# Another unit order for one token group, weight splits moved beside it, and an output block in two halves

## The chip, the cores and the metric

The kernel runs on one core of a Trainium2 chip, all in one launch. The metric is the device time of that launch in microseconds. Beside the times there is one profiled execution, with a trace of every engine: TensorE (PE, its weight loads PEld), VectorE (DVE), ScalarE (ACT), GpSimd (POOL) and the DMA queue of SyncE (SP).

## What is computed

The reference, cut to what matters (float32 in and out; 1152 tokens, 512 features):

```python
x = attention(q, k, v)                 # 2 x 8 heads, 576 positions, 32 keys per query (every 4th for half the heads)
h = x @ w_in                           # MoE1: 512 -> 2048
g = h * np.tanh(np.log1p(np.exp(h)))
x = g @ w_out                          # 2048 -> 512
p = domain_probs / domain_probs.sum(-1, keepdims=True)
for e in range(4):                     # MoE2: four experts, 512 -> 1024 -> 512
    out += p[:, e:e + 1] * (np.maximum(x @ w1[e], 0) @ w2[e])
```

## The kernel before

Every matrix product is done in three matmuls: each operand is split into a high part (`hi`, an ACT copy to the matmul's float format) and the rest (`lo`, a subtraction), and hi·hi, hi·lo and lo·hi are added up in PSUM. A **split** is thus one ACT instruction and one subtraction on DVE or POOL (`split`, L541 to L543).

**Attention** ends about 90 us in and isn't touched.

**MoE1** has 16 units; a unit `u` is 128 columns of `w_in` with the 128 rows of `w_out` that belong to them, 1024 columns of hi and of lo. They are decoded and split while token group 0 runs (`dec_dve`, `dec_act`) and then stay in SBUF: units 0 to 3 in `wxh`/`wxl`, unit 4 in `late[0:2]`, units 5 to 15 one behind the other in `late[2:4]` (11264 columns). Tokens come in three groups of 512, 320 and 320. Group 0 has one unit in a step, groups 1 and 2 have two. A step (`Step1`) is `first` (24 matmuls of L497, into banks 6 and 7), `act` (the Mish, ACT L502), `split` (ACT L505, DVE L506) and `second` (24 matmuls of L517, into four banks kept for the whole group). The loop at L830 emits, for each step i, `first` of i, `second` of i - 1, then `act` and `split` of i, and then what the table `beside` lists for it: splits that MoE2 will need. NSB is the number of the first step of group 2, its last is NSB + 7. `y_out` copies a group's four banks out, in turn on ACT and DVE.

**MoE2** computes x·w1 by a scheme with 7 products in place of 8 (A11·B11, S1·T1, S2·T2, ...: sums of blocks of w1, and of x). An expert's weights come in four pairs (`p`), each 256 hidden columns. A pair is prepared by

- `prep_a`: splits of A12 and A22 (ACT 512 and 256 wide, DVE), then four POOL sums in place (L654 to L657),
- `prep_s`: split of the four sums (ACT 1024 wide, DVE), then the load of the next pair's w1,
- `prep_w2`: split of w2 (ACT 1024 wide, POOL), then the load of the next pair's w2.

The result takes 2816 columns of `late[2:4]`, pair p from column 2816·p on, so over MoE1's units: pair 0 over units 5 to 7, pair 1 over 7 to 10, pair 2 over 10 to 13, pair 3 over 13 to 15. Expert 0's pairs can be written only where group 2 has already used those units. The staging buffers `stage1` (w1) and `stage2` (w2) hold one pair each.

Work on tokens goes by `Group`: expert e, token set j (256 or 320 columns a product), pair p. `first_a` runs five of the products, `mid` and `first_b` the rest with Relu and split, `second` multiplies by w2 into `accs`, banks 1 to 4 or 1 to 5, which are kept over the four pairs, and `finish` (after pair 3) adds prob times the bank to the output rows (DVE L764) and stores them (SP L766). Products use three banks: a, b, c, which are 6, 7, 0. In `first_a`, ACT copies bank a away (L710, L714) before the next product goes into it:

```python
            self.prod(self.a, "A11", "B11", True)
            self.prod(self.b, "S1", "T1", True)
            ACT.activation(p1, self.a, AF.Copy)
            ACT.activation(self.cb[:, 2 * N:3 * N], self.b, AF.Copy)
            self.prod(self.a, "S2", "T2")
```

The loop at L856 emits for group i: `first_a`, the first half of `second` of group i - 1 (for i = 0 MoE1's last `second` and `y_out(2)`), `mid`, the work in `slots[i, 0]`, `first_b`, the second half of that `second`, the work in `slots[i, 1]`. Nothing reorders what is emitted: each engine takes its instructions in this order. The last group's `second` stands at the end (L873 to L878): per output block of 128 tokens six matmuls, then `finish` of the block.

Of the kernel before, what the change touches and what calls it, by code (L numbers as in the profile page):

```python
# [23 lines left out]
def kernel(  # L24
# [13 lines left out]
    PE, ACT, DVE, POOL, SP = nc.tensor, nc.scalar, nc.vector, nc.gpsimd, nc.sync  # L38
# [3 lines left out]
    DM = out.shape[1]  # L42
    NT = B * S
    NE = w1.shape[0]
    NF1 = w_in.shape[1] // 128
    NF2 = w1.shape[2] // 128
    NUA = 4
# [15 lines left out]
    def nm(s):  # L63
        uid[0] += 1
        return f"{s}{uid[0]}"

    def bank(n):
        return ps.tile([128, 512], F32, tag=f"bank{n}", name=nm("bank"))
# [158 lines left out]
    for lo in (0, 32):  # L227
        m = msk[lo:lo + 32, :]
# [23 lines left out]
    t = bank(7)  # L252
# [223 lines left out]
    yacc = {}  # L476

    class Step1:
# [29 lines left out]
        def second(self):  # L508
            if self.grp not in yacc:
                yacc[self.grp] = [bank(b)[:, 0:self.w] for b in ((0, 1, 2, 3), (4, 5, 0, 1), (2, 3, 4, 5))[self.grp]]  # L510
            for i, u in enumerate(self.us):
                wh, wl = units[u]
                g = slice(self.w * i, self.w * (i + 1))
                for d in range(4):
                    s = slice(512 + 128 * d, 640 + 128 * d)
                    for k, (a, x) in enumerate(((wh, self.ghi), (wl, self.ghi), (wh, self.glo))):
                        PE.matmul(yacc[self.grp][d], a[:, s], x[:, g], start=u == 0 and k == 0,  # L517
                                  stop=u == NF1 - 1 and k == 2)

    steps = [Step1(f, 0, [f]) for f in range(NF1)]  # L520
    NSA = len(steps)
    for g in (1, 2):
        for f in range(0, NF1, 2):
            steps.append(Step1(len(steps), g, [f, f + 1]))
    NS1 = len(steps)
    NSB = (NSA + NS1) // 2

# [25 lines left out]
    NP2 = NF2 // 2  # L553
# [43 lines left out]
    def set0_t42(k):  # L597
        h, l, o = ((xh, xl, 1536), (wxh, wxl, 1024))[k]
        split(h[:, o:o + 512], l[:, o:o + 512], rawf[1][:, 512 * k:512 * k + 512], DVE)
# [4 lines left out]
    def set1_b(m):  # L604
        o = slice(xb + 2 * n1 * m, xb + 2 * n1 * (m + 1))
        split(xh[:, o], xl[:, o], y1[(0, 1, 3)[m]], DVE)
# [20 lines left out]
    def pair_at(n):  # L627
        return divmod(n, NP2) if n < NE * NP2 else None
# [7 lines left out]
    def load_w2(n):  # L636
        if pair_at(n):
            e, p = pair_at(n)
            SP.dma_start(out=stage2.rearrange("p (h d) -> p h d", h=2),
                         in_=w2[e, 256 * p:256 * (p + 1), :].rearrange("(h p) d -> p h d", p=128))  # L640
# [5 lines left out]
    def prep_a(n):  # L646
        o = PW * (n % NP2)
        r = stage1.rearrange("p (c f m) -> p c f m", c=4, f=2)
        a12 = [w[:, o:o + 512].rearrange("p (c m) -> p c m", c=4) for w in late[2:4]]
        a22 = [w[:, o + 512:o + 768].rearrange("p (c m) -> p c m", c=2) for w in late[2:4]]  # L650
        split(*a12, r[:, :, 0], DVE)
        split(*a22, r[:, 2:4, 1], DVE)
        a11, a12, a21, a22 = blocks()
        POOL.tensor_tensor(out=a22, in0=a21, in1=a22, op=ALU.add)  # L654
        POOL.tensor_tensor(out=a21, in0=a11, in1=a21, op=ALU.subtract)
        POOL.tensor_tensor(out=a11, in0=a22, in1=a11, op=ALU.subtract)
        POOL.tensor_tensor(out=a12, in0=a12, in1=a11, op=ALU.subtract)  # L657

    def prep_s(n):
        o = PW * (n % NP2) + 768  # L660
        split(late[2][:, o:o + 1024], late[3][:, o:o + 1024], stage1, DVE)
        load_w1(n + 1)
        ready.add(("s", n))

    def prep_w2(n):
        o = PW * (n % NP2) + 1792
        split(late[2][:, o:o + 1024], late[3][:, o:o + 1024], stage2, POOL)
        load_w2(n + 1)
        ready.add(("w2", n))
# [8 lines left out]
    class Group:  # L678
# [22 lines left out]
        def first_a(self):  # L701
            assert ("s", self.e * NP2 + self.p) in ready
            N = self.N
            self.a, self.b, self.c = (bank(m)[:, 0:N] for m in (6, 7, 0))
            self.cb = rawf[2][:, 0:3 * N]
            p1, u2 = (late[4][:, 320 * i:320 * i + N] for i in range(2))
            self.u2 = u2
# [5 lines that stand above are left out]
            self.prod(self.c, "A12", "B21", True)  # L713
            ACT.activation(u2, self.a, AF.Copy)  # L714
            self.prod(self.a, "S3", "T3")
            DVE.tensor_tensor(out=self.cb[:, 0:N], in0=self.c, in1=p1, op=ALU.add)  # L716
            DVE.tensor_tensor(out=self.cb[:, 2 * N:3 * N], in0=self.a, in1=self.cb[:, 2 * N:3 * N], op=ALU.add)
# [25 lines left out]
        def second(self, f, which=slice(None)):  # L743
            assert ("w2", self.e * NP2 + self.p) in ready
            o = PW * self.p + 1792 + 512 * f
            wh, wl = (w[:, o:o + 512] for w in late[2:4])
            hi, lo = self.g[f]
            for acc, t, cols in self.accs()[which]:
                s = slice(128 * t, 128 * t + 128)
                for i, (x, a) in enumerate(((hi, wh), (hi, wl), (lo, wh))):  # L750
                    PE.matmul(acc, x[:, s], a[:, cols], start=self.p == 0 and f == 0 and i == 0,  # L751
                              stop=self.p == NP2 - 1 and f == 1 and i == 2)

        def finish(self, which=slice(None)):
            if self.p != NP2 - 1:
# [32 lines left out]
    for s in range(-2, NA - 2):  # L788
# [32 lines left out]
              NSA + 2: [lambda: set0_b("B22"), set0_sums, normalise_prob],  # L821
              NSA + 4: [lambda: set0_t42(0)],
              NSB + 1: [set0_t13, lambda: load_w1(0)],
              NSB + 2: [lambda: set0_t42(1), lambda: load_w2(0)],
              NSB + 3: [lambda: set1_b(0), lambda: set1_b(1)],
              NSB + 4: [lambda: prep_a(0)],
              NSB + 5: [lambda: prep_s(0), lambda: prep_w2(0)],
              NSB + 6: [lambda: prep_a(1)],
              NSB + 7: [lambda: prep_s(1), lambda: prep_w2(1)]}
    for i in range(2, NS1):  # L830
        if i > 2:
            steps[i].first()
# [8 lines left out]
    for e in range(NE):  # L841
        for j in range(2):
            for p in range(NP2):
                groups.append(Group(len(groups), e, j, p))
    NG2 = len(groups)

    slots = {(0, 0): [lambda: prep_a(2)], (0, 1): [lambda: prep_s(2), lambda: prep_w2(2)],
             (1, 0): [lambda: prep_a(3)], (1, 1): [lambda: prep_s(3), lambda: prep_w2(3)],
             (2, 0): [lambda: set1_b(2), lambda: set1_sums(0)], (2, 1): [lambda: set1_sums(1), lambda: set1_t("T1")],
             (3, 0): [lambda: set1_t("T3"), lambda: set1_t("T4")], (3, 1): [lambda: set1_t("T2")]}  # L850
    for e in range(1, NE):
        for p in range(NP2):
            n, g = e * NP2 + p, 2 * NP2 * (e - 1) + NP2 + p + 1
# [17 lines left out]
        for do in slots.get((i, 1), ()):  # L871
            do()
    g = groups[-1]  # L873
    n = len(g.accs())
    for t in range(n):
        for f in range(2):
            g.second(f, slice(t, t + 1))
        g.finish(slice(t, t + 1))  # L878
# [32 lines left out]
```

## Time and profile before

| | us |
|---|---|
| three runs | 669.08, 670.16, 671.54 (median 670.16) |
| the profiled execution, its own time | 668.4 |
| its span, first to last instruction | 666.6 |
| TensorE busy | 636.1 |
| DVE, ACT, POOL busy | 290.3, 275.3, 158.8 |
| mean granted clock of TensorE | 0.994 of 2.4 GHz |

The span is what the trace shows; the rest of the execution's own time lies around it. Busy times are of one engine each and overlap. A matmul's row lasts longer than the distance to the next one, since they are pipelined; how fast TensorE goes is read from the distance of the starts. A wait is shown in square brackets behind the instruction that had to wait, with what ended it.

### The profile page before, as it was taken

Reading aid. Unit: us, or ns where it says so; the run is one execution under the profiler, and the core shown is the slowest. Engines: PE = TensorE matmul, PEld = TensorE weight load, DVE = VectorE, ACT = ScalarE, POOL = GpSimd, SP = SyncE. Lnnn points to the kernel's source line nnn. Section 1 sums busy time; section 2 is a strip of 40 time slices with the busy share of each in tenths; the row PEclk is TensorE's granted clock in tenths of the full one; section 3 lists DMA queues with packets and bytes.
Section 4 is the critical chain, followed back from the end, with each engine's and each line's share of the span. In section 5 each row is a group of like instructions: output and inputs, shape, how many; then the busy total and the mean of one; then the engine's idle time right before and its main releaser. Section 6 shows DMA issues by size and latency. Waiting matters only on the chain.

```text
span 666.6 us, 10149 instructions
## 1 busy us (share of the span) xinstructions
PE 636.1 (95%) x4148; PEld 564.7 (85%) x4148; DVE 290.3 (44%) x490; ACT 275.3 (41%) x553; POOL 158.8 (24%) x170
## 2 busy tenths in 40 slices
PE   7676899999999999979999999999999999999997
PEld 4455678888999999969998889998889998898986
DVE  3577876661311223345444452444632544623323
ACT  7797666662322234443244432334422344322210
POOL 8011245550300003345033410043400134300000
PEclk9998999999999999989999999999999999999999
DMA  9999356640000012222003210021210022000102
GB/s 182 221 205 206 98 160 190 188 126 0 1 1 1 1 64 64 64 63 64 1 32 94 64 64 1 0 64 64 64 63 1 1 78 85 28 1 1 63 1 79
DMA packets 47310, 45.82 MB, mean 69 GB/s; under 512 B 12192, under 2 KB 39968, under 8 KB 47264
## 3 DMA queue, kind: packets, MB, share of 16 engines
q1 hardware_dynamic: 47264, 45.18, 25.6%
q8 instruction: 32, 0.52, 0.3%
q14 instruction: 14, 0.11, 0.1%
HBM read 42.81 MB, written 2.36 MB: 68 GB/s over the span
## 4 chain that ended last, share of the span: by engine, by line
PE 86%; ACT 4%; POOL 3%; DMA 2%; DVE 2%; issue 1%; SPq 0%; POOLq 0%; ACTq 0%; DVEq 0%
PE bank L751 30%; PE bank L698 27%; PE bank L517 14%; PE bank L497 14%; DMA raw<-in_moe_w_in_dram 1%; DMA nat<-in_q_dram 1%; ACT qkD L338 1%; ACT qkP L338 1%; ACT xh L420 1%; POOL vP L205 1%; POOL vD L212 0%; PE bank L320 0%; DVE xl L424 0%; DVE scr L150 0%; ACT pr L365 0%
## 5 line engine op out<-in xcount | busy, mean ns | idle before, releaser
L698 PE MATMUL bank<-xh,late 128*128 128x256 f32 (+1 forms) x512 | 121.1, 298 | 5.0 <-ACT late L710 3.6
L698 PEld LDWEIGHTS bank<-xh,late 128*128 128x128 f32 x512 | 88.6, 188 | 9.5 <-ACT late L710 5.1
L698 PE MATMUL bank<-wxh,late 128*128 128x320 f32 (+1 forms) x384 | 95.3, 298 | 0.0
L751 PE MATMUL bank<-late,gh 128*128 128x512 f32 x288 | 89.8, 393 | 0.0
L497 PE MATMUL bank<-xh,late 128*128 128x320 f32 (+1 forms) x288 | 76.3, 338 | 0.0
L698 PE MATMUL bank<-xl,late 128*128 128x256 f32 (+1 forms) x256 | 75.5, 295 | 0.0
L517 PE MATMUL bank<-gh,late 128*128 128x320 f32 (+1 forms) x288 | 72.6, 338 | 0.0
L654 POOL TENSOR_TENSOR raw<-raw 128x256 f32<-128x256 f32 x16 | 11.7, 734 | 238.4 <-DVE late L543 238.4
L698 PEld LDWEIGHTS bank<-wxh,late 128*128 128x128 f32 x384 | 68.3, 189 | 0.0
L506 DVE TENSOR_TENSOR gl<-scr,gh 128x512 fp32r<-128x512 f32 (+1 forms) x32 | 25.0, 780 | 88.7 <-ACT gh L505 88.7
L751 PEld LDWEIGHTS bank<-late,gh 128*128 128x128 f32 x288 | 52.8, 190 | 9.7
L502 ACT ACTIVATE scr<-bank 128x320 f32<-128x320 f32 (+1 forms) x48 | 23.4, 492 | 88.1 <-PE bank L497 88.1
L716 DVE TENSOR_TENSOR raw<-bank,late 128x256 f32<-128x256 f32 (+1 forms) x32 | 14.6, 457 | 101.2 <-PE bank L698 94.1
L751 PE MATMUL bank<-late,gl 128*128 128x512 f32 x144 | 57.0, 396 | 0.0
L698 PE MATMUL bank<-wxl,late 128*128 128x256 f32 (+1 forms) x192 | 56.6, 295 | 0.0
L542 ACT ACTIVATE late<-raw 128x512 fp32r<-128x512 f32 (+1 forms) x64 | 48.2, 783 | 19.9 <-PE bank L751 16.8
L497 PEld LDWEIGHTS bank<-xh,late 128*128 128x128 f32 x288 | 50.7, 188 | 4.3
L517 PEld LDWEIGHTS bank<-gh,late 128*128 128x128 f32 x288 | 50.1, 188 | 4.2
L751 PE MATMUL bank<-late,late 128*128 128x512 f32 x216 | 52.6, 391 | 0.0
L543 POOL TENSOR_TENSOR late<-raw,late 128x1024 fp32r<-128x1024 f32 x16 | 38.7, 2419 | 57.1 <-ACT late L542 57.1
L698 PEld LDWEIGHTS bank<-xl,late 128*128 128x128 f32 x256 | 48.3, 189 | 2.5
L497 PE MATMUL bank<-xl,late 128*128 128x320 f32 (+1 forms) x144 | 48.6, 338 | 0.0
(140 smaller groups left out, 1164.1 us busy)
## 6 DMA issues: line engine op xcount, KB each, us to landing
raw<-in_moe_w_dram SPq DMA_DIRECT2D x32, 512.0 KB, 3.5
raw<-in_moe_w_in_dram SPq DMA_DIRECT2D x16, 512.0 KB, 4.1
raw<-in_moe_w_out_dram SPq DMA_DIRECT2D x16, 512.0 KB, 3.6
out_dram<-scr SPq DMA_DIRECT2D x9, 256.0 KB, 2.1
nat<-in_k_dram SPq DMA_DIRECT2D x8, 256.0 KB, 5.6
nat<-in_q_dram SPq DMA_DIRECT2D x8, 256.0 KB, 6.2
vD<-in_v_dram SPq DMA_DIRECT2D x8, 192.0 KB, 7.0
vP<-in_v_dram SPq DMA_DIRECT2D x8, 160.0 KB, 6.5
```

The costliest lines, as they stand in the source:

```text
L205: POOL.memset(vP[64 * j:64 * j + 64, :, blk, 1 - j, :], 0.0)
L338: ACT.activation(*move(g, par, j), AF.Copy)
L497: PE.matmul(h, a[:, c, :], x[:, c, :], start=c == 0 and k == 0, stop=c == 3 and k == 2)
L502: ACT.activation(self.hc[:, self.w * i:self.w * (i + 1)], h, AF.Mish)
L506: DVE.tensor_tensor(out=self.glo, in0=self.hc, in1=self.ghi.bitcast(F32), op=ALU.subtract)
L517: PE.matmul(yacc[self.grp][d], a[:, s], x[:, g], start=u == 0 and k == 0, stop=u == NF1 - 1 and k == 2)
L542: ACT.activation(hi, src, AF.Copy)
L543: eng.tensor_tensor(out=lo, in0=src, in1=hi.bitcast(F32), op=ALU.subtract)
L654: POOL.tensor_tensor(out=a22, in0=a21, in1=a22, op=ALU.add)
L698: PE.matmul(out, w, x(k), start=first and k == 0 and i == 0, stop=k == 1 and i == 2, skip_group_check=not first)
L716: DVE.tensor_tensor(out=self.cb[:, 0:N], in0=self.c, in1=p1, op=ALU.add)
L751: PE.matmul(acc, x[:, s], a[:, cols], start=self.p == 0 and f == 0 and i == 0, stop=self.p == NP2 - 1 and f == 1 and i == 2)
```

## The change

Four things are changed. Token group 2 takes its units in the order 0, 1, 5 to 15, 2, 3, 4, so that `late[2:4]` comes free from the front two steps earlier (the `start` and `stop` of the accumulation follow that order). Pairs 0, 1 and 2 of MoE2 are prepared in the steps NSB + 2 to NSB + 7 instead of pairs 0 and 1 in NSB + 4 to NSB + 7; pair 3 goes to `slots[0, 1]` and `slots[1, 1]`; the two splits `set1_b` go from one step to two others. Group 1 (n = 1) has bank 5 for its bank a. And the last output block is accumulated, finished and stored in two column halves.

```diff
-                        PE.matmul(yacc[self.grp][d], a[:, s], x[:, g], start=u == 0 and k == 0,
-                                  stop=u == NF1 - 1 and k == 2)
-
-    steps = [Step1(f, 0, [f]) for f in range(NF1)]
+                        PE.matmul(yacc[self.grp][d], a[:, s], x[:, g], start=u == UORD[self.grp][0] and k == 0,
+                                  stop=u == UORD[self.grp][-1] and k == 2)
+    UORD = [list(range(NF1)), list(range(NF1)), [0, 1, *range(NUA + 1, NF1), *range(2, NUA + 1)]]
+    steps = [Step1(f, 0, [f]) for f in UORD[0]]
...
-            steps.append(Step1(len(steps), g, [f, f + 1]))
+            steps.append(Step1(len(steps), g, UORD[g][f:f + 2]))
...
-            self.a, self.b, self.c = (bank(m)[:, 0:N] for m in (6, 7, 0))
+            self.a, self.b, self.c = (bank(m)[:, 0:N] for m in (5 if self.n == 1 else 6, 7, 0))
...
-              NSB + 2: [lambda: set0_t42(1), lambda: load_w2(0)],
-              NSB + 3: [lambda: set1_b(0), lambda: set1_b(1)],
-              NSB + 4: [lambda: prep_a(0)],
-              NSB + 5: [lambda: prep_s(0), lambda: prep_w2(0)],
-              NSB + 6: [lambda: prep_a(1)],
-              NSB + 7: [lambda: prep_s(1), lambda: prep_w2(1)]}
+              NSB + 2: [lambda: set0_t42(1), lambda: load_w2(0), lambda: prep_a(0)],
+              NSB + 3: [lambda: prep_s(0), lambda: prep_w2(0)],
+              NSB + 4: [lambda: prep_a(1), lambda: set1_b(0)],
+              NSB + 5: [lambda: prep_s(1), lambda: prep_w2(1), lambda: set1_b(1)],
+              NSB + 6: [lambda: prep_a(2)],
+              NSB + 7: [lambda: prep_s(2), lambda: prep_w2(2)]}
...
-    slots = {(0, 0): [lambda: prep_a(2)], (0, 1): [lambda: prep_s(2), lambda: prep_w2(2)],
-             (1, 0): [lambda: prep_a(3)], (1, 1): [lambda: prep_s(3), lambda: prep_w2(3)],
+    slots = {(0, 1): [lambda: prep_a(3)], (1, 1): [lambda: prep_s(3), lambda: prep_w2(3)],
...
-    n = len(g.accs())
-    for t in range(n):
+    accs = g.accs()
+    acc, t, _ = accs.pop()
+    accs += [(acc[:, c], t, c) for c in (slice(0, DM // 2), slice(DM // 2, DM))]
+    for t in range(len(accs)):
```

Lines 698, 710, 722, 732, 764 and 766 of the kernel before are 700, 712, 724, 734, 767 and 769 of the changed one.

How the instructions move is shown at three places. The first is ACT from `y_out(2)`'s last copy (L537) to p1 of group 1 (L710), before (`raw0` is stage1, `raw1` stage2, `late2` the hi parts, `late4` holds p1):

```order
L537 ACTIVATE scr_75<-bank168_2206 128x320
L721 ACTIVATE gh_68<-raw2_72 128x256
L542 ACTIVATE late2_1154<-raw0_70 128x512
L542 ACTIVATE late2_1154<-raw0_70 128x256
L721 ACTIVATE gh_68<-bank182_2598 128x256
L721 ACTIVATE gh_68<-raw2_72 128x512
L542 ACTIVATE late2_1154<-raw0_70 128x1024
L542 ACTIVATE late2_1154<-raw1_71 128x1024
L710 ACTIVATE late4_1156<-bank185_2697 128x256
```

And the same stretch now:

```order
L539 ACTIVATE scr_75<-bank168_2206 128x320
L723 ACTIVATE gh_68<-raw2_72 128x256
L723 ACTIVATE gh_68<-bank182_2612 128x256
L723 ACTIVATE gh_68<-raw2_72 128x512
L544 ACTIVATE late2_1154<-raw0_70 128x512
L544 ACTIVATE late2_1154<-raw0_70 128x256
L712 ACTIVATE late4_1156<-bank185_2705 128x256
```

The four splits of pair 2 that stood between group 0's results and p1 are gone; the two of `prep_a(3)`, which stood behind p1, stand right ahead of it. On DVE, L732 likewise no longer stands behind two subtractions of `prep_a`.

The second place is ACT in step NSB + 3 (the Mish of its two units, the split of g, and what `beside` adds), before:

```order
L502 ACTIVATE scr_75<-bank172_2296 128x320
L502 ACTIVATE scr_75<-bank173_2309 128x320
L505 ACTIVATE gh_68<-scr_75 128x640
L542 ACTIVATE xh_64<-scr_75 128x640 x2
L502 ACTIVATE scr_75<-bank174_2354 128x320
```

And now:

```order
L502 ACTIVATE scr_75<-bank172_2304 128x320
L502 ACTIVATE scr_75<-bank173_2317 128x320
L505 ACTIVATE gh_68<-scr_75 128x640
L544 ACTIVATE late2_1154<-raw0_70 128x1024
L544 ACTIVATE late2_1154<-raw1_71 128x1024
L502 ACTIVATE scr_75<-bank174_2364 128x320
```

The two `set1_b` splits made room for `prep_s(0)`, which follows POOL's sums, and `prep_w2(0)`; the next step's Mish is behind them.

The third place is the end of TensorE's program now, with the waits, from the last matmul of the block before (bank306 and bank307 are the banks of the last two output blocks):

```order
L753 MATMUL bank306_5338<-late2_1154,late1_1153 128x512
L753 MATMUL bank307_5339<-late2_1154,wxh_66 128x256
L753 MATMUL bank307_5339<-late3_1155,wxh_66 128x256
L753 MATMUL bank307_5339<-late2_1154,wxl_67 128x256
L753 MATMUL bank307_5339<-late2_1154,late0_1152 128x256
L753 MATMUL bank307_5339<-late3_1155,late0_1152 128x256
L753 MATMUL bank307_5339<-late2_1154,late1_1153 128x256
L753 MATMUL bank307_5339<-late2_1154,wxh_66 128x256 [waits DVE_49]
L753 MATMUL bank307_5339<-late3_1155,wxh_66 128x256
```

The six matmuls of 512 columns became twice six of 256, and the seventh waits for DVE, whose `finish` of the first half (L767) reads the same bank.

## Rows read from the trace of the kernel before

**Rows 1.** The page, part 1: busy us (share) and instructions of each engine.

```profile
PE 636.1 (95%) x4148; PEld 564.7 (85%) x4148; DVE 290.3 (44%) x490; ACT 275.3 (41%) x553; POOL 158.8 (24%) x170
```

**Rows 2.** Waits of PE: who waited for whom, us in total, times, longest.

```profile
PE bank L698 <- ACT late L710: 3.6, 1, 3.6
```

**Rows 3.** Timeline of PE, 283 to 289: start, us, instruction [idle before].

```profile
283.55 0.38 PE L698 MATMUL bank<-xh,late 128*128 128x256 f32 x1 [1.27 <-DVE gl L722]
...
284.90 0.28 PE L698 MATMUL bank<-wxh,late 128*128 128x256 f32 x1
...
288.78 0.39 PE L698 MATMUL bank<-xh,late 128*128 128x256 f32 x1 [3.61 <-ACT late L710]
```

**Rows 4.** The chain of waits, 268 to 312: start, us, what.

```profile
288.78 3.34 PE bank L698 x18
292.12 3.36 PE bank L751 x12
...
299.61 3.65 PE bank L698 x30
```

**Rows 5.** Windows: length, busy PE, PEld, DVE, ACT, POOL, granted clock, DMA share, GB/s.

```profile
290.00:291.00 1.00, 1.00 (x6) 1.00 (x6) 0.06 (x1) 0.18 (x1) 1.00 (x1) 0.50 0.86 282
165.00:175.00 10.00, 9.36 (x61) 8.79 (x60) 4.15 (x6) 4.65 (x9) 1.51 (x1) 1.00 0.01 2
664.40:665.20 0.80, 0.00 (x0) 0.00 (x0) 0.00 (x0) 0.00 (x0) 0.00 (x0) 1.00 0.87 328
```

**Rows 6.** Timeline of DVE, 280.9 to 283.

```profile
280.94 0.49 DVE L539 COPY scr<-bank 128x320 f32<-128x320 f32 x1 [0.39 <-PE bank L517]
...
281.80 1.03 DVE L543 TENSOR_TENSOR late<-raw,late 128x512 fp32r<-128x512 f32 x2
282.74 0.41 DVE L732 TENSOR_TENSOR raw<-bank,late 128x256 f32<-128x256 f32 x1
```

**Rows 7.** Timeline of ACT, 281 to 289.

```profile
281.14 0.93 ACT L542 ACTIVATE late<-raw 128x512 fp32r<-128x512 f32 x2
282.31 0.38 ACT L721 ACTIVATE gh<-bank 128x256 fp32r<-128x256 f32 x1 [0.24 <-PE bank L698]
283.19 0.63 ACT L721 ACTIVATE gh<-raw 128x512 fp32r<-128x512 f32 x1 [0.50 <-DVE raw L732]
286.46 2.00 ACT L542 ACTIVATE late<-raw 128x1024 fp32r<-128x1024 f32 x2 [2.63 <-POOL raw L657]
288.37 0.36 ACT L710 ACTIVATE late<-bank 128x256 f32<-128x256 f32 x1
```

**Rows 8.** Timeline of ACT beside token group 2, 243 to 251.

```profile
243.26 1.35 ACT L542 ACTIVATE xh<-scr 128x640 fp32r<-128x640 f32 x2
247.43 0.44 ACT L502 ACTIVATE scr<-bank 128x320 f32<-128x320 f32 x1 [2.82 <-PE bank L497]
...
250.30 0.92 ACT L542 ACTIVATE late<-raw 128x512 fp32r<-128x512 f32 x2
```

**Rows 9.** Timeline of POOL, 252 to 255: first and last of four sums.

```profile
252.27 0.74 POOL L654 TENSOR_TENSOR raw<-raw 128x256 f32<-128x256 f32 x1 [69.00 <-DVE late L543]
...
254.73 0.74 POOL L657 TENSOR_TENSOR raw<-raw 128x256 f32<-128x256 f32 x1
```

**Rows 10.** Timeline of SP's queue, 232 to 233.

```profile
232.21 0.37 SPq L633 DMA_DIRECT2D raw<-in_moe_w_dram  x1
```

**Rows 11.** DMA issues (w1 and w2; output): count, KB each, us to landing.

```profile
raw<-in_moe_w_dram SPq DMA_DIRECT2D x32, 512.0 KB, 3.5
...
out_dram<-scr SPq DMA_DIRECT2D x9, 256.0 KB, 2.1
```

**Rows 12.** Timeline of DVE, 661 to 663.

```profile
661.41 0.75 DVE L764 SCALAR_TENSOR_TENSOR scr<-bank,prob,scr 128x512 f32<-128x512 f32 x1 [0.64 <-PE bank L751]
662.81 0.75 DVE L764 SCALAR_TENSOR_TENSOR scr<-bank,prob,scr 128x512 f32<-128x512 f32 x1 [0.64 <-PE bank L751]
```

**Rows 13.** Timeline of PE, 661.1 to 663: the last block's first matmuls.

```profile
661.21 0.63 PE L751 MATMUL bank<-late,wxh 128*128 128x512 f32 x2
```

More of the change, by code (lines that the diff above doesn't have):

```diff
@@ L751, in second @@
                     PE.matmul(acc, x[:, s], a[:, cols], start=self.p == 0 and f == 0 and i == 0,
-                              stop=self.p == NP2 - 1 and f == 1 and i == 2)
+                              stop=self.p == NP2 - 1 and f == 1 and i == 2,
+                              skip_group_check=self.n >= NG2 - NP2 and t == self.rows - 1)
         def finish(self, which=slice(None)):
```

## The prediction

> **What bounds the kernel now.** I read the busy times on the profile's page first: TensorE is busy 636.1 of 666.6 us [rows 1], so time can only be won where it stands, where its clock is low, or behind its last matmul. The waits of TensorE come second: from the first MoE step to the end, the longest one is for an ACT copy, 3.6 us in one piece [rows 2]. The timeline of TensorE places it [rows 3]: in the first two groups of MoE2, TensorE waits 1.27 us for a DVE subtraction (until 283.55) and 3.61 us for the copy p1 of L710 (until 288.78). The chain of waits says what the stretch after that costs [rows 4], and the windows show why: the granted clock is 0.50 in it, 1.2 instead of 2.4 GHz [rows 5].
>
> Why those two waits are there is told by ACT and DVE, which take their instructions in the order written. Pair 2 of MoE2's weights is prepared between group 0's results. On DVE the two subtractions of prep_a(2) (1.03 us) stand ahead of L732, which so starts at 282.74 [rows 6]; ACT's 512-wide Relu copy waits for L732 until 283.19 and DVE's subtraction from bank 6 stands behind it too, and group 1's first product needs bank 6. On ACT the splits of prep_s(2) and prep_w2(2) (2.00 us) wait 2.63 us for POOL's last sum, start at 286.46, and L710 stands behind them at 288.37 [rows 7]. TensorE can't write S2·T2 into the bank that L710 has yet to copy.
>
> **The change, part by part.**
>
> *The unit order of token group 2.* TensorE's matmuls keep number and shape (24 and 24 per step); only which weights they read changes. I cost it at nothing: the weights of all 16 units have been in SBUF since group 0.
>
> *The three preparations beside group 2.* Moved to earlier places on the queues: per pair four ACT splits, three DVE and one POOL subtraction, four POOL sums and two loads on SP, 14 instructions, the loads included; pair 0 and 1 go two steps earlier, pair 2 leaves group 0. Their cover is ACT's idle time before the next Mish. A step is 7.04 us (243.26 to 250.30) [rows 8]. In the step that held the two set1_b splits (1.35 us), ACT still idled 2.82 us before the next Mish [rows 8]. With prep_s and prep_w2 there (2.00 us [rows 7]) 2.82 + 1.35 - 2.00 = 2.17 us are left; with one set1_b more (0.68), 1.49 us. The wait it adds: prep_s stands on ACT and waits for POOL's sums, with the next Mish, and so TensorE, behind it. For pair 0, the sums ran from 252.27 to 255.47 [rows 9]; two steps earlier (14.08), behind one 512-wide split (0.6), they end near 255.47 - 14.08 + 0.6 = 242.0. ACT comes to prep_s at 243.3, so it doesn't wait, and it could wait 2.17 us more before a Mish is late. The load of pair 0's w1 is issued at 232.21 [rows 10] and lands 3.5 us later [rows 11], at 235.7, a microsecond before prep_a(0) asks for it at 236.7. The later loads follow their buffers' release and have nothing queued behind them on SP but each other. Cost: 0.
>
> *Group 0 and 1.* Without prep_a(2) on DVE, L732 follows at once, near 281.8, and bank 7 is free in time. Group 1's first product now goes into bank 5, which y_out's last copy leaves at 280.94 + 0.49 = 281.43 [rows 6]; TensorE is there at 283.55 - 1.27 = 282.28 by the end of its last matmul (0.28 long, issued every 0.12: 30 in 3.65 [rows 3, 4]), so at 282.12 by its issue. The wait of 1.27 us goes. Twelve matmuls later, at 282.12 + 12 x 0.12 = 283.55, TensorE wants bank 5 back, and what is late next is again p1: on ACT it stands behind the Relu of bank 6 (starts 282.31, 0.38), the 512-wide one (0.63) and now the pair of prep_a(3) (0.93), with 0.36 of its own [rows 7]. That sums to 284.61; neighbours on ACT overlap by about 0.1 (286.46 + 2.00 = 288.46, but L710 starts at 288.37), three times, so 284.3, and TensorE goes 0.05 later (288.73 to 288.78 [rows 3, 7]), at 284.35. That is **4.43 us** earlier than 288.78. The bounds: 284.66 without the overlaps, and 283.55 if ACT needed no time, 4.1 to 5.2 us. What was queued behind prep_a(3) before, prep_s(3) and its POOL sums, gets more room: TensorE has 24 more matmuls of group 0 to do by then.
>
> *The clock.* From 288.78, 18 matmuls took 3.34 us, where 30 take 3.65 (so 18 take 2.19), and 12 512-wide ones 3.36 [rows 4], where six take 1.40 (the last blocks' spacing, 661.41 to 662.81 [rows 12]) and so 12 take 2.80. That is 1.15 + 0.56 = **1.7 us**. The half clock came a microsecond after 4.9 us of standing in 6.5. In its place I expect one stand of 0.8 us, and the trace has one like it, in the stretch 165 to 175, where TensorE stood 0.64 us with the granted clock 1.00 throughout [rows 5]. So I take the 1.7 as gained; the other end is nothing.
>
> *The last block in halves.* Its matmuls (twelve of 256 columns in place of six of 512) take 12 x 0.12 = 1.44 for 1.40, and six weight loads more hide beside them as everywhere. But both halves lie in one bank, and the order shows the second half's first matmul waiting for DVE, whose read of the first half it follows. The block starts at 661.21 [rows 13]. First half issued by 661.94 and done 0.16 later; DVE is free at 661.41 + 0.75 = 662.16 [rows 12] and takes about 0.42 (a 128x256 operation takes 0.41 [rows 6]; the upper bound is the full 0.75); TensorE resumes at 662.63, needs 0.73 + 0.16 + 0.1 for a restart, and DVE ends at 664.07, where it ended at 663.56 before: 0.5 us later. The last store moves half as much: its data took some 0.7 of 2.1 us (the 0.8 us window at 0.87 share [rows 5, 11]), so 0.36 is saved; bounds 0 and 0.72. Sum: **+0.15 us**, between -0.2 and +1.2.
>
> Here a row and a rule part. While DVE reads one block, TensorE writes the next at full rate, the blocks being 1.40 apart with DVE's 0.75 inside [rows 12]; by that the halves would overlap as well, DVE would end 0.33 earlier, and the tail would give -0.33 - 0.36 = -0.7 us. The Trainium skill (PSUM — Partial Sum Buffer, Terms) says that TensorE writing and VectorE reading the same bank and quadrant at once is an error; no run so far shows that. By that rule the wait can't be done without, and the tail is the +0.15 of the sum.
>
> *Sum:* -4.43 - 1.7 + 0.15 = **-6.0 us**. The profiled execution took 668.4 us, so 662.4; it lies 1.8 under the median of the three runs (670.16, from 669.08 to 671.54), and from the median the same gain gives **664.2 us**, which is what I forecast.
>
> **The rivals.** *The clock falls all the same.* For it: the one fall in the MoE stages followed on waits at this very place, and 0.8 us is a little longer than 0.64. Against: [rows 5]. Then 664.2 + 1.7 = 665.9 us.
>
> *The halves overlap* (the last step does in full what its name says). For it: the blocks do [rows 12]. Against: the wait in the order. Then 664.2 - 0.8 = 663.4 us.
>
> *The preparation holds up MoE1* and the kernel is slower, or at best unchanged. Place: prep_s on ACT in the steps beside group 2, waiting for POOL's sums with the Mish behind it. It decides from the point where the sums end 3.4 us later than worked out above (242.0 against 243.3 + 2.17), so where they take twice their 3.2 us; what goes beyond it enters TensorE's time three times. At three times 3.2 us it is 3 x (6.4 - 3.4) = 9.0 us, with a clock fall 10.7, less the gain of 6.0: 674.9 us. In between, the gain is just eaten. For it: more of POOL's and DVE's work now falls together. Against: the same sums beside the same kind of step took 0.82 us apiece [rows 9].
>
> **How the numbers follow.** Forecast 0.76, clock falls 0.11, halves overlap 0.05, preparation eats the gain 0.05, preparation slower 0.03. About 0.5% (3.35 us) is what a measurement of this kernel tells from no change. The first three cases lie beyond it; I move 0.05 of them to no change for the spread of the runs, which is 1.4 us upward: faster 0.87, same 0.10, slower 0.03. The range goes down to 661.8 (the forecast with no new wait, 663.4, and 1.6 of the 1.8 that the profiled run lies under the median) and up to 667.2 (the clock falls, 665.9, and 1.3 of spread).
>
> **What would show it.** TensorE's waits: the 1.27 us for DVE gone, the 3.61 us for ACT L712 (the old L710) at 0.5 to 0.9, and no wait of L497 for ACT between 225 and 274; granted clock 1.00 around 285 to 292. In the tail, TensorE waits some 0.5 us for L767 before the last six matmuls, and the final DVE row is half as long. I am wrong if TensorE waits for Mish (L502) beside group 2, if p1 of group 1 comes later than 285, or if the clock is at 0.50 after it.

## The result and the profile after

The changed kernel takes **665.21 us** (median of 6 runs, 663.41 to 666.99); the kernel before, run beside it, 671.75 (6 runs with the three shown ahead, 669.08 to 673.15). The ratio is 0.9908 [0.9881, 0.9936]: 6.5 us or 0.9% faster. The forecast was 664.2 us, 6.0 less than the median that was known then.

The profiled execution took 663.83 us, its span is 662.1, and the mean granted clock 0.995. Over the whole span TensorE is busy 1.2 us longer than in [rows 1]; that hides the change, and the split by stages below shows it.

```profile
PE 637.3 (96%) x4154; PEld 566.2 (86%) x4154; DVE 290.9 (44%) x491; ACT 274.9 (42%) x553; POOL 158.4 (24%) x170
```

**How the two traces are compared.** Attention doesn't take the same time twice: the first matmul of MoE2 in the chain stands between 273.79 us (before) and 280.16 us in the traces of this study. So I count each trace from fixed points. From the first matmul of MoE1's first full step (12 matmuls of L497) to the first matmul of MoE2 it takes 186.43 us before (87.36 to 273.79) and 186.43 after (88.43 to 274.86). From there to the end of the span (666.60 before, 662.05 after) it takes 392.81 us before and 387.19 after, **5.62 less**. A second run of the same kernel (a1_change_again, below; span 665.90) has 186.42 and 386.81, 6.00 less. The 0.4 us between these two traces of one kernel build up over all of MoE2 in steps of up to 0.1, so a smaller effect can't be read from the length of the whole stage; where one is claimed below, it is read from pieces of it. The spans alone differ by only 4.55, since attention was 1.07 longer in the trace of after; the medians of the runs differ by 6.5.

The busy time by stages: up to MoE1's first full step TensorE is busy 67.06 us before and 69.82 after, in MoE1 185.04 in both, and from MoE2's first matmul on 383.97 before and 382.43 after. So of the 5.62 us, 1.54 are busy time, won by the clock, and 4.08 are standing time.

Waits of TensorE after (who waited for whom, us in total, times, longest), the ones of MoE2:

```profile
PE bank L700 <- ACT late L712: 0.7, 1, 0.7
PE bank L753 <- DVE scr L767: 0.6, 1, 0.6
```

The wait of 1.27 us for DVE [rows 3] is gone, the one of 3.61 us [rows 2, 3] has become 0.68, and the tail has the new one. The timeline around that place (start, us, instruction, idle before and what ended it), first TensorE's:

```profile
285.47 0.39 PE L700 MATMUL bank<-xh,late 128*128 128x256 f32 x1 [0.68 <-ACT late L712]
```

ACT's in the same stretch:

```profile
283.42 0.38 ACT L723 ACTIVATE gh<-bank 128x256 fp32r<-128x256 f32 x1 [1.11 <-PE bank L700]
283.70 0.62 ACT L723 ACTIVATE gh<-raw 128x512 fp32r<-128x512 f32 x1
284.22 0.93 ACT L544 ACTIVATE late<-raw 128x512 fp32r<-128x512 f32 x2
285.04 0.37 ACT L712 ACTIVATE late<-bank 128x256 f32<-128x256 f32 x1
```

And DVE's, from y_out's last copy on:

```profile
282.00 0.49 DVE L541 COPY scr<-bank 128x320 f32<-128x320 f32 x1 [0.39 <-PE bank L517]
...
282.74 0.42 DVE L734 TENSOR_TENSOR raw<-bank,late 128x256 f32<-128x256 f32 x1
```

Counted from MoE2's first matmul, TensorE comes back at 285.47 - 274.86 = 10.61 us, where it was 288.78 - 273.79 = 14.99 before: 4.38 earlier. ACT's four instructions stand back to back, as the sum had them, and L734 starts 0.74 us after the start of y_out's last copy, where L732 started 1.80 after it [rows 6].

The chain after (start, us, what), over the pieces that answer to [rows 4]:

```profile
274.86 3.58 PE bank L700 x30
...
285.04 0.38 ACT late L712
285.43 0.04 issue
285.47 2.41 PE bank L700 x18
287.88 2.75 PE bank L753 x12
```

A window over the same stretch (columns as in [rows 5]):

```profile
285.47:292.00 6.53, 6.53 (x43) 6.04 (x44) 2.49 (x6) 1.02 (x3) 2.96 (x4) 1.00 0.00 0
```

The 18 matmuls take 2.41 us instead of 3.34, the 12 wide ones 2.75 instead of 3.36, together 1.54 less, and the granted clock is 1.00 (2.4 GHz) where it was 0.50 (1.2 GHz) before.

ACT's timeline beside token group 2, around the step that answers to [rows 8]:

```profile
244.33 2.00 ACT L544 ACTIVATE late<-raw 128x1024 fp32r<-128x1024 f32 x2
248.49 0.44 ACT L502 ACTIVATE scr<-bank 128x320 f32<-128x320 f32 x1 [2.17 <-PE bank L497]
```

And POOL's there, the last of the four sums:

```profile
242.30 0.73 POOL L659 TENSOR_TENSOR raw<-raw 128x256 f32<-128x256 f32 x1
```

POOL's last sum ends at 243.03, 1.3 us before ACT comes to prep_s, and ACT still idles 2.17 us before the next Mish. That is the number worked out ahead, and the stage didn't change its length.

The tail in TensorE's timeline, the first matmuls of either half:

```profile
656.26 0.41 PE L753 MATMUL bank<-late,wxh 128*128 128x256 f32 x2
...
657.72 0.50 PE L753 MATMUL bank<-late,wxh 128*128 128x256 f32 x2 [0.58 <-DVE scr L767]
```

DVE's two last entries (x2 joins the block before and the first half):

```profile
656.46 1.20 DVE L767 SCALAR_TENSOR_TENSOR scr<-bank,prob,scr 128x512 f32<-128x512 f32 x2 [0.64 <-PE bank L753]
658.73 0.48 DVE L767 SCALAR_TENSOR_TENSOR scr<-bank,prob,scr 128x256 f32<-128x256 f32 x1 [1.07 <-PE bank L753]
```

The last block's first matmul is at 656.26, DVE ends at 659.21, 2.95 us later; before it was 661.21 to 663.56, 2.35 [rows 12, 13]. From DVE's end to the end of the span it is 2.84 after and 3.04 before. The tail is 0.40 us longer (5.79 against 5.39).

### The profile page after: what moved, and what is told of

It reads as the page before. It is cut to its first block, busy times and chain, and to the rows that moved or that the text cites. A ratio compares the mean times of both kernels' runs of the same rounds, so it can differ in the third digit from the quotient of the medians.

```text
span 662.1 us, 10164 instructions
## 1 busy us (share of the span) xinstructions
PE 637.3 (96%) x4154; PEld 566.2 (86%) x4154; DVE 290.9 (44%) x491; ACT 274.9 (42%) x553; POOL 158.4 (24%) x170
## 4 chain that ended last, share of the span: by engine, by line
PE 88%; ACT 4%; DMA 3%; DVE 2%; issue 1%; SPq 1%; ACTq 0%; DVEq 0%
PE bank L753 30%; PE bank L700 27%; PE bank L517 15%; PE bank L497 14%; DMA nat<-in_q_dram 2%; DMA raw<-in_moe_w_in_dram 1%; PE bank L320 1%; ACT qkD L338 1%; ACT qkP L338 1%; ACT xh L420 1%; ACT pT L382 0%; DVE scr L150 0%; DVE xl L424 0%; ACT pr L365 0%; PE bank L377 0%
## 5 line engine op out<-in xcount | busy, mean ns | idle before, releaser
L753 PE MATMUL bank<-late,gh 128*128 128x512 f32 x288 | 89.2, 391 | 0.0
L497 PE MATMUL bank<-xh,late 128*128 128x320 f32 (+1 forms) x288 | 76.6, 338 | 0.7 <-ACT scr L502 0.7
L753 PEld LDWEIGHTS bank<-late,gh 128*128 128x128 f32 x288 | 52.3, 188 | 9.7
L753 PE MATMUL bank<-late,gl 128*128 128x512 f32 x144 | 56.7, 394 | 0.0
L497 PEld LDWEIGHTS bank<-xh,late 128*128 128x128 f32 x288 | 50.7, 188 | 5.3 <-ACT scr L502 1.0
L753 PE MATMUL bank<-late,late 128*128 128x512 f32 (+1 forms) x219 | 52.8, 388 | 0.0
L497 PE MATMUL bank<-xl,late 128*128 128x320 f32 (+1 forms) x144 | 48.6, 338 | 0.0
```

The source lines that it names most:

```text
L497: PE.matmul(h, a[:, c, :], x[:, c, :], start=c == 0 and k == 0, stop=c == 3 and k == 2)
```

## The experiments

Each is told by its stage of MoE2 (first matmul of MoE2 in the chain to the end of the span, here to a tenth; before 392.8, the change 387.2 and 386.8), and by the ratio of medians with its interval where it was timed against the kernel before. MoE1, counted as above, is 186.42 to 186.44 us in all of them but the last. A run told as one run has one trace and no interval.

**e1_bank5_alone.** The kernel before with bank 5 for group 1 alone, to tell whether its two waits are two costs.

```diff
-            self.a, self.b, self.c = (bank(m)[:, 0:N] for m in (6, 7, 0))
+            self.a, self.b, self.c = (bank(m)[:, 0:N] for m in (5 if self.n == 1 else 6, 7, 0))
```

> The kernel before, with bank 5 for group 1's bank a and nothing else. Theory (the two waits of TensorE are one: it stands until ACT has copied p1, which the splits of prep_s(2) hold up): the 1.27 us wait for DVE goes, the wait for ACT L710 grows from 3.61 to about 4.9 us, p1 stays near where it was, the clock still falls, and from the first matmul of MoE2 to the end it takes 392.8 us as before (within 0.3). Rival (each wait costs its own length): 1.3 us less, 391.5.

Measured: ratio 1.0023 [0.9999, 1.0047], MoE2 392.8. TensorE's waits in MoE2:

```profile
PE bank L698 <- ACT late L710: 4.6, 1, 4.6
...
PE bank L698 <- DVE raw L732: 0.2, 1, 0.2
```

The wait of 1.27 is gone, the other is 1.0 longer, and a short one for L732 is new; TensorE comes back 14.99 us after MoE2's first matmul (291.59 - 276.60), as in the kernel before to the hundredth. Two waits in series on one end are one cost: the end is set by ACT, and bank 5 alone takes nothing off it. The granted clock falls here too, and it falls while TensorE still stands: it is 0.67 between 289 and 290 and 0.50 from 290 to 296. In the kernel before it was still 1.00 when TensorE came back, 0.94 between 289 and 290, and then 0.50 [rows 5].

**e2_order_alone.** The kernel before with the new unit order alone (UORD, all else as before).

```diff
-            steps.append(Step1(len(steps), g, [f, f + 1]))
+            steps.append(Step1(len(steps), g, UORD[g][f:f + 2]))
```

> The kernel before, with the unit order of token group 2 and nothing else. Theory (the order alone costs and gives nothing, it only frees columns): token group 2's steps still 7.04 us each, the waits of 1.27 and 3.61 us and the clock fall as before, 392.8 us from the first matmul of MoE2 on, within 0.3. Rival (part of the gain comes from the order itself): the steps or what follows are over 1 us shorter.

Measured: 671.26 us, ratio 1.0 [0.9979, 1.0022], MoE2 392.2, the same two waits (1.2 and 3.6 us). MoE2 is 0.6 shorter than in the trace before, which misses the expected 392.8 within 0.3; the difference builds up over the whole stage, as it does between the two traces of the change, and the ratio shows none. So no run shows that the order costs or brings anything by itself: it makes room for the preparations. The stretch after the wait differs (start, us, what):

```profile
291.35 3.53 PE bank L699 x18
294.88 3.16 PE bank L752 x12
```

By the 2.41 and 2.75 of the same pieces at full clock the fall costs 1.53 us here, 1.54 in the kernel before, and 2.05 in e1 (4.21 and 3.00).

**e3_no_bank5.** The change with bank 6 for group 1 again.

```diff
-            self.a, self.b, self.c = (bank(m)[:, 0:N] for m in (5 if self.n == 1 else 6, 7, 0))
+            self.a, self.b, self.c = (bank(m)[:, 0:N] for m in (6, 7, 0))
```

> The change without bank 5 (group 1 keeps bank 6). Theory (with p1 setting the end of the wait, bank 5 is worth little): TensorE waits about 1.0 us for DVE L724 ahead of A11, then only some 0.1 us or nothing for ACT L712, and MoE2 takes 387.2 + 0.2 to 0.4 us. Rival (each wait costs its own length): 387.2 + 1.0 us or more, the wait of 0.68 us staying.

Measured: 666.34 us, ratio 0.9914 [0.9885, 0.9943], MoE2 387.0. TensorE's timeline where it waits:

```profile
287.90 0.39 PE L700 MATMUL bank<-xh,late 128*128 128x256 f32 x1 [0.93 <-DVE gl L724]
```

A window of what follows (columns as in [rows 5]):

```profile
287.90:294.00 6.10, 6.10 (x41) 5.64 (x42) 2.90 (x6) 2.40 (x7) 2.96 (x4) 1.00 0.00 0
```

And the chain behind it (start, us, what):

```profile
291.81 2.75 PE bank L753 x12
```

TensorE waits 0.93 us for DVE before its first product of group 1, and ACT's p1 is then no longer late. That wait is 0.25 us longer than the one with bank 5, and from MoE2's first matmul (278.45) to these twelve of L753 it takes 13.36 us, where both traces of the change have 13.02: bank 5 is worth about a third of a microsecond. The whole stage doesn't show it: its 387.0 lies between the two traces of the change, and below the 387.4 to 387.6 that were expected. After 0.93 us of standing the clock is at 1.00.

**e4_whole_block.** The change with the last block whole.

```diff
     accs = g.accs()
-    acc, t, _ = accs.pop()
-    accs += [(acc[:, c], t, c) for c in (slice(0, DM // 2), slice(DM // 2, DM))]
```

> The change with the last output block whole. Theory (the halves cost by the wait for DVE in between): the 0.58 us wait goes, the last DVE row ends 2.35 us after the block's first matmul in place of 2.95, and from the first matmul of MoE2 to the end it takes 0.2 to 0.6 us less than 387.2. Rival (the smaller last store gives back more than the wait costs): 0.1 to 0.4 us more than 387.2.

Measured: 663.79 us (4 runs), ratio 0.9891 [0.9853, 0.9929], MoE2 386.5. DVE's last row:

```profile
657.74 0.75 DVE L767 SCALAR_TENSOR_TENSOR scr<-bank,prob,scr 128x512 f32<-128x512 f32 x1 [0.64 <-PE bank L753]
```

From the last block's first matmul to DVE's end it is 2.34 us again, to the end of the span 5.39 (before 5.39, the change 5.79). The halves cost 0.40 us.

**e5_pair2_late.** The change with pair 2 prepared in MoE2 again, save its prep_a: TensorE then waits longer at the same place.

```diff
               NSB + 6: [lambda: prep_a(2)],
-              NSB + 7: [lambda: prep_s(2), lambda: prep_w2(2)]}
...
-    slots = {(0, 1): [lambda: prep_a(3)], (1, 1): [lambda: prep_s(3), lambda: prep_w2(3)],
+    slots = {(0, 1): [lambda: prep_s(2), lambda: prep_w2(2)], (1, 0): [lambda: prep_a(3)],
+             (1, 1): [lambda: prep_s(3), lambda: prep_w2(3)],
```

> The change with prep_s(2) and prep_w2(2) back in slot (0, 1), their sums still made early, and prep_a(3) in slot (1, 0). Theory (TensorE's stand is what ACT has in front of p1, and the clock fell because of the long stand): ACT has 2.00 us of splits in front of p1 in place of 0.93, without a wait for POOL, so TensorE waits about 1.7 us for ACT L712 in place of 0.68; the granted clock stays 1.00 after it; from MoE2's first matmul to the end 1.0 us more than with the change (386.9 to 387.2), so 387.9 to 388.2. Rival (a fall of the clock comes with any stand over a microsecond at this place): 0.50 for some us after it and up to 1.7 us more, 389.6 to 389.9.

Measured (one run): 666.06 us, MoE2 389.8. TensorE's timeline at that place:

```profile
286.15 0.39 PE L700 MATMUL bank<-xh,late 128*128 128x256 f32 x1 [1.75 <-ACT late L712]
```

The windows after it (columns as in [rows 5]):

```profile
286.15:287.00 0.85, 0.85 (x6) 0.85 (x7) 0.00 (x0) 0.22 (x1) 0.85 (x1) 0.93 0.00 0
287.00:288.00 1.00, 1.00 (x7) 1.00 (x6) 0.00 (x0) 0.38 (x1) 1.00 (x1) 0.50 0.68 183
...
290.00:291.00 1.00, 1.00 (x5) 0.86 (x4) 0.52 (x2) 0.65 (x2) 0.00 (x0) 0.85 0.71 276
291.00:292.00 1.00, 1.00 (x6) 0.79 (x5) 0.90 (x3) 0.59 (x2) 0.00 (x0) 1.00 0.48 184
```

And the chain there (start, us, what):

```profile
286.15 3.63 PE bank L700 x18
289.78 3.09 PE bank L753 x12
```

My theory on the clock failed here, and what the rival said came about. After this one stand of 1.75 us, within 0.85 us of TensorE's return the grant began to fall (0.93 in the first window), it was 0.50 in the next, and back at 1.00 by 291. It cost (3.63 - 2.41) + (3.09 - 2.75) = 1.56 us, and the longer wait 1.75 - 0.68 = 1.07, together the 2.6 by which MoE2 is longer than in the change's first trace (3.0 against its second).

The length of a stand alone doesn't decide it, though. The same trace has longer ones in attention (who waited for whom, us in total, times, longest):

```profile
PE bank L320 <- DMA nat<-in_q_dram: 5.4, 4, 2.9
...
PE bank L389 <- ACT pT L382: 3.7, 3, 2.5
```

These two stands of 2.94 and 2.48 us end at 32.16 and 76.48, and the mean granted clock from 0 to 88.05, where MoE1's first full step begins, is 1.00. What makes the difference isn't shown, nor whether a stand of 1.75 us at this place is always followed by a fall: it was tried once.

**e6_pair3_later.** The change with prep_a(3) one slot later, behind the copy p1.

```diff
-    slots = {(0, 1): [lambda: prep_a(3)], (1, 1): [lambda: prep_s(3), lambda: prep_w2(3)],
+    slots = {(1, 0): [lambda: prep_a(3)], (1, 1): [lambda: prep_s(3), lambda: prep_w2(3)],
```

> The change with prep_a(3) in slot (1, 0), behind group 1's p1 instead of ahead of it. Theory (the wait of 0.68 us that is left is ACT's pair of prep_a(3) splits): no wait of TensorE for ACT L712, 0.7 to 0.8 us less from MoE2's first matmul to the end than with the change (386.9 to 387.2), so 386.1 to 386.5; prep_s(3) still doesn't wait long enough to hold up group 2. Rival (it only moves: POOL's sums come later, ACT waits for them at prep_s(3), and TensorE for group 2's p1): a new wait of TensorE for ACT L712 of 0.5 us or more after 290, and no gain.

Measured (one run): 665.41 us, MoE2 386.7. TensorE's timeline one group later than the wait that was removed:

```profile
297.91 0.39 PE L700 MATMUL bank<-xh,late 128*128 128x256 f32 x1 [0.50 <-ACT late L712]
```

ACT's ahead of it:

```profile
295.58 2.01 ACT L544 ACTIVATE late<-raw 128x1024 fp32r<-128x1024 f32 x2 [1.35 <-POOL raw L659]
297.50 0.36 ACT L712 ACTIVATE late<-bank 128x256 f32<-128x256 f32 x1
```

The rival was right in the main: the wait of 0.68 for p1 of group 1 is gone, and the p1 of the next group is late in its place, since prep_s(3) on ACT now waits for POOL's sums, with p1 behind it. The gain is 0.15 us (from MoE2's first matmul to the twelve of L753 behind this wait 23.40, in the change 23.55). It is the pattern of the kernel before, in small.

**e7_halves_apart.** The change with the whole block before it put between the two halves.

```diff
-    accs += [(acc[:, c], t, c) for c in (slice(0, DM // 2), slice(DM // 2, DM))]
+    halves = [(acc[:, c], t, c) for c in (slice(0, DM // 2), slice(DM // 2, DM))]
+    accs[-1:] = [halves[0], accs[-1], halves[1]]
```

> The change with the order of the last three pieces turned: first half of the last block, then the whole block before it, then the second half. Theory (the two halves only cost because they follow each other in one bank): no wait of TensorE for DVE L767, DVE ends about 1.9 to 2.0 us after the start of these last two blocks' second one (2.35 with the whole block, 2.95 with the halves one after the other), and 0.9 to 1.1 us less to the end than with the change, so 385.8 to 386.3 from MoE2's first matmul. Rival (DVE's last operations and the stores are what ends the kernel): DVE's queue or the stores take the gain and it is under 0.4 us.

Measured (one run): 665.13 us, MoE2 386.3. DVE's last entry (the whole block and the second half joined):

```profile
659.08 1.20 DVE L767 SCALAR_TENSOR_TENSOR scr<-bank,prob,scr 128x512 f32<-128x512 f32 x2 [0.92 <-PE bank L753]
```

The small stores in the DMA view of the tail (count, KB each, median us to landing):

```profile
out_dram<-scr SPq DMA_DIRECT2D x2, 128.0 KB, 2.0
```

The same stores in the change:

```profile
out_dram<-scr SPq DMA_DIRECT2D x2, 128.0 KB, 1.8
```

TensorE's wait in the tail is gone. From the first matmul of the last two blocks to DVE's end it takes 3.52 us (656.76 to 660.28), 4.35 in the change (654.86 to 659.21), 3.74 before (659.82 to 663.56). Of these 0.83 some 0.24 are given back: the span ends 3.08 after DVE, where it was 2.84, and no store landed within less than 1.9 us, the fastest small one of the change within 1.7. The last one follows a store of 256 KB by half a microsecond, which may be the reason; no run tells. The expectation had left that out. From the same matmul to the end of the span it is 6.60 us, 7.19 in the change and 6.78 before: 0.59 less than the change, where 0.9 to 1.1 was expected, and 0.2 less than with a whole last block. The three kernels below that keep the halves apart have 6.59 or 6.60.

**e8_both.** e6 and e7 together.

> Both of the last two: prep_a(3) behind p1 and the halves apart. Theory: the two gains lie at different places on TensorE's path and add up, 1.7 us less than with the change from MoE2's first matmul on, 385.1 to 385.5, no wait of TensorE in MoE2 over 0.3 us, and a ratio to the kernel before of about 0.988 (the change: 0.9908). Rival (they don't add up): 386 or more.

Measured: 664.85 us (5 runs), ratio 0.9893 [0.9874, 0.9912], MoE2 386.1. The expected 385.1 to 385.5 is missed, and the number is the rival's (386 or more), but not for its reason: the wait of 0.50 for p1 stays, as in e6. In pieces both gains are there, 23.40 us to the same twelve of L753 as in e6 and 6.60 from the last two blocks' first matmul to the end as in e7, so they add; e6's is small.

**a1_change_again.** The change once more, beside the two that follow.

> The change itself once more, as the measure for the others. Theory (what differs between runs of one kernel lies in attention, before MoE1's steady part): from the 12 matmuls of L497 with which the steady part begins to MoE2's first matmul 186.4 us, as in all runs so far; from there to the end 386.8 to 387.3; the waits of 0.68 us for ACT L712 and 0.58 us for DVE L767. Rival (the stages after attention vary as much as the whole): 186.4 or 387 missed by over 1 us.

Measured (one run): 667.95 us, MoE2 386.8, the waits of 0.68 and 0.58 as in the first. MoE2 began at 279.09 us, 4.2 later than in the first trace of the same kernel, and MoE1's first full step at 92.67: what differs by microseconds between runs lies ahead of MoE1.

**e10_pair3_spread.** e8 with prep_s(3) and prep_w2(3) later and apart, so that nothing waits for POOL ahead of p1.

```diff
-    slots = {(0, 1): [lambda: prep_a(3)], (1, 1): [lambda: prep_s(3), lambda: prep_w2(3)],
-             (2, 0): [lambda: set1_b(2), lambda: set1_sums(0)], (2, 1): [lambda: set1_sums(1), lambda: set1_t("T1")],
+    slots = {(1, 0): [lambda: prep_a(3)],
+             (2, 0): [lambda: prep_s(3), lambda: set1_b(2), lambda: set1_sums(0)],
+             (2, 1): [lambda: prep_w2(3), lambda: set1_sums(1), lambda: set1_t("T1")],
```

> The kernel with prep_a(3) behind p1 and the halves apart, and now prep_s(3) in slot (2, 0) and prep_w2(3) in slot (2, 1), so that what waits for POOL's sums stands behind group 2's p1 as well. Theory (the 0.50 us wait for ACT L712 in group 2 is prep_s(3) waiting 1.36 us for POOL): no wait of TensorE for ACT L712 over 0.2 us, 386.1 - 0.5 = 385.5 to 385.8 us from MoE2's first matmul. Rival (the work has to stand somewhere and holds up a later copy): a new wait in groups 2 to 4, and 386 or more.

Measured (one run): 668.02 us with MoE2 beginning at 280.16; MoE2 385.8, 1.0 less than the change beside it. No wait in MoE2 is left in TensorE's list, and the chain over the place that had the first of them is matmuls without a gap, 42 in one piece:

```profile
283.75 3.52 PE bank L517 x24
287.27 5.08 PE bank L700 x42
292.35 2.80 PE bank L753 x12
```

**e11_mish_first.** e10, and in MoE1 the copies of y_out emitted behind the Mish of the same step instead of ahead of it.

```diff
+        step1_act(i)
         if i in (NSA, NSB):
...
-        step1_act(i)
```

> The same, and in MoE1 y_out behind the Mish and split of the step beside it instead of ahead of them (the two waits of 0.7 us of L497 for ACT L502, at the two changes of token group, are of the same kind: what TensorE waits for stands on ACT behind copies that wait for TensorE). Theory: both waits go, from the start of the steady part to MoE2's first matmul 1.6 to 2.0 us less than 186.4; MoE2 as in the run with pair 3 spread; ratio to the kernel before 0.985 to 0.987. Rival (the copies, now later, hold up the banks that the next group's sums go into): a wait of L517 for ACT or DVE in their place, and 186 us or more.

Measured: **662.60 us** (6 runs, 658.67 to 663.98), ratio **0.986 [0.9828, 0.9892]**; MoE1 184.49, 1.93 less, MoE2 385.4. The waits list of the change has, in MoE1, twice:

```profile
PE bank L497 <- ACT scr L502: 1.4, 2, 0.7
```

That wait is gone in e11, where of MoE1's waits only a short one for DVE is left, which the change has too (0.4 us):

```profile
PE bank L517 <- DVE gl L506: 0.5, 1, 0.5
```

The 24 matmuls of L497 behind each of the two waits took 3.78 us in the change's chain; no 24 of L497 around there take more than 3.52 here, which is about the rest of the 1.93. It is the same fault as at MoE2's start: copies that could wait stood on ACT ahead of a Mish that TensorE waits for. This median is the lowest of all; the intervals of the two ratios, of this kernel and of the change, overlap a little (0.9881 to 0.9892).

## Why the prediction was right, and where it wasn't

| term | forecast | measured |
|---|---|---|
| TensorE back at group 1's second product | -4.43 | -4.38 |
| clock in the stretch behind it | -1.7 | -1.54 |
| MoE1 with three preparations beside it | 0 | 0.00 |
| tail | +0.15 | +0.40 |
| MoE2 and the tail together | -6.0 | -5.6 and -6.0 (two traces) |

The measured rows add up to -5.52; what the traces have beyond that is of the size by which two traces of the change differ in this stage.

*The waits* were right in size and in mechanism. The sum of ACT's queue up to p1 (the Relu copies, the pair of prep_a(3), p1 itself, less the overlaps) was 0.05 us off, and the wait that takes the old one's place was put at 0.8 and is 0.68. e1 and e3 show which edit brings it: bank 5 without the moved preparations brings nothing, the moved preparations without bank 5 nearly all.

*The cover in MoE1* held to the hundredth (2.17 us of ACT's idle time left), and POOL was ahead of ACT. The rival of a preparation that holds up the Mish never came near its point.

*The clock* came out as forecast and its worth nearly so (1.54 for 1.7; the 18 matmuls took 2.41 us at the full clock, not the 2.19 taken), but the reasoning was thinner than its chance of 0.11 against it said. It rested on one stand of 0.64 us without a fall, set against 4.9 us of standing with one, and left out the stands in attention, where the trace of the kernel before has one of 2.99 us (28.9 to 31.9) with the granted clock at 1.00. e3 shows no fall after 0.93 us at this place, e5 one after a single stand of 1.75. With ACT's queue ahead of p1 a microsecond longer, as in e5, the fall came back, and with it the rival's 1.6 us; that the change stays clear of it is in part luck, since where the limit lies isn't known.

*The tail* is the term that was mis-sized, within its bounds. The part of DVE's end went about as worked out (+0.60 for +0.5; the 256-wide operation reading a bank took 0.45 to 0.48 us, not the 0.42 taken). The part of the store, 0.36 us saved, came out too large: the half stores land in 1.8 us at the median, whole ones in 2.1 [rows 11], and from DVE's end to the end of the span only 0.20 is saved; where the rest goes isn't shown. So this part of the change makes the kernel slower, by 0.40 us (e4), which the forecast had as +0.15. The wait that causes it is the one on the bank: the order holds TensorE off while DVE reads the other half, 0.58 us in the trace. Put apart, the halves do gain, 0.2 us against a whole last block (e7).

The Trainium skill (DMA: Bandwidth & Descriptors, Anatomy of one DMA — SWDGE (gpsimd) path) gives a transfer a fixed part of about 2.0 us and 436 GB/s behind it, for transfers that GpSimd issues; by that, halving 256 KB saves an estimated 0.3 us. The saving is near what the stores show (2.1 to 1.8 us at the median), the fixed part is not: on SP's queue the whole transfer of 128 KB took less than 2.0 in the change. The rule of the Trainium skill (PSUM — Partial Sum Buffer, Terms) that the prediction weighed was never put to the test, since the order kept TensorE behind DVE's read of the bank in every kernel that has the halves; whether they could share it without that wasn't tried.

*The 6.5 us of the medians* against the 5.6 and 6.0 of the traces: the stages that the change touches give the latter, and the remainder is of the size by which attention differs from run to run. What makes attention differ isn't shown, but the clock is a candidate: up to MoE1's first full step the mean granted clock was 1.00 in e5, 0.98 before and 0.96 after, where that step starts at 88.05, 87.36 and 88.43 us, and 0.93 in a1 and 0.91 in e3 and e10, where it starts at 92.67, 92.02 and 93.74. Single traces don't follow that order (e4: 0.92 and 88.64).

## What to carry to other kernels

When a fast engine waits for a small copy, read what stands ahead of that copy on its own in-order queue, and what that in turn waits for; then work out the new time of the copy from that queue instruction by instruction. Two waits one behind the other on the same chain are one cost, and removing the first alone only lengthens the second (e1); a moved instruction can bring the wait back one group later (e6). Splitting a last piece in halves cost time here when the halves followed each other in one bank (0.40 us, e4) and gained a little with other work between them (0.2 us, e7); and where an earlier stage varies by more than the effect, compare the stages from fixed points in the trace.

## What the runs showed that was not expected

A single stand of 1.75 us in otherwise unbroken matmuls was followed by a fall of the granted clock to 0.50 for some 3 us and cost 1.56 us (e5), nearly as much as the wait itself, while stands of 2.48 and 2.94 us in attention, in the same trace, were followed by none. The price of such a fall was 1.5 to 2.1 us at the same place in different runs (before, e1, e2). MoE1's length from its first full step repeats to 0.02 us between runs that leave its order alone, while its start lies anywhere from 87.36 to 93.74 (before, e10). And a store of half the size landed 0.3 us sooner (median 1.8 against 2.1), but hardly sooner in e7 (2.0), where the last one follows a whole store closely.
